# Folding w_phi into wk and wq in groups of six heads instead of row chunks, with a new order of work

## The chip, the cores and the metric

The kernel runs on one core of one Trainium2 chip. A core has TensorE (PE; its weight loads are listed apart as PEld), VectorE (DVE), ScalarE (ACT), GpSimd (POOL) and SyncE (SP), and 16 DMA engines. The metric is the device time of one execution in microseconds. Three executions of the kernel before took 286.2, 286.44 and 286.89 us: a median of 286.44 us.

## The reference, cut to what matters

One token-mixing block and one feed-forward block work on the same x (2048 tokens, D = 640) and are mixed by a gate. The first block is a linear attention with H = 32 heads of Dh = 20 columns:

```
q, k, v = split(x @ wqkv)                          # heads of 20 columns
pq, pk  = q @ w_phi[h],  k @ w_phi[h]              # per head, 20 x 20
phi_q   = [softmax(pq), softmax(-pq)]              # 40 columns a head
phi_k   = [softmax(pk), softmax(-pk)]
kv, z   = sum over tokens of phi_k^T v, of phi_k
a       = (phi_q kv / (phi_q z + 1e-6)) @ wo
b       = (silu(x @ w_gate) * (x @ w_up)) @ w_down # F = 1728
out     = g * a + (1 - g) * b,   g = sigmoid(sum(x * gate_w))
```

Since (x wk) w_phi = x (wk w_phi), with w_phi laid out as a block-diagonal matrix of 32 blocks, the kernel first multiplies wk and wq with w_phi (the "premult") and then needs one projection a token tile in place of two. The change is about this premult.

## The kernel before, in words

Everything is in bf16 with sums in f32. The tokens are 16 tiles of 128 and 4 batches of 4 tiles. The program has no planner at run time: two strings, LOADS and ORDER, list short names of operations, and a loop at the end of `_build` (L849) calls them in that order. Every engine gets its instructions in the order in which they are called; `_Tracker` (L54) adds the semaphore waits that reads and writes of the same bytes need. SP issues nearly all DMAs, in order, and so does ACT for a few.

The names that matter:

- `x`, `t` load token tiles: x0 to x3 as rows, which TensorE transposes (`X`), t4 to t15 by a transposing DMA into xT. `w` loads wv, `f` the FFN weights in three column parts (0 to 256, 256 to 896, 896 to 1728), `h` loads w_phi into the tile wph (from ACT's queue, once the fourth wv load has landed).
- `k0` to `k4`, `q0` to `q4` (`load_wt`, L406) load wk and wq transposed: chunk m is rows 128m to 128m+127 of wqkv, all 640 columns of k (or q), and becomes five blocks [128 columns x 128 rows] in wT (wTq for q).
- `Y` (`w_blocks`, L578) builds the block-diagonal matrix wbd from wph and the mask bmask. As 128 is no multiple of 20, a chunk of 128 rows cuts through heads: each of the five chunks of wbd has 160 columns (8 heads of which some belong partly to the next chunk), and neighbouring chunks overlap. POOL does chunks 0, 2, 4, DVE chunks 1, 3.
- `M0` to `M4` for k and `R0` to `R4` for q (`premult`, L584): six matmuls for a chunk m of rows, one for each entry of BANDS (L573): the weights are a block of wT, 128x128, what moves is a part of wbd, 140 columns in four of the six and 80 in the other two. The result, 640 columns, is copied from PSUM to wqk in one copy: by DVE for M0 and M3, by ACT for the others.
- `V` projects a token tile to v and the gate (`U` is a fifth of a V, for the first three tiles); `K` and `Q` project it to k and q with wqk (10 matmuls of 320 columns), and ACT makes exp(+) and exp(-) of it. A K or a Q reads all five row chunks of wqk, so it needs all five premults.
- `S`, `P` normalise the exponentials of a K tile (DVE: sums and reciprocals; POOL: the multiplication); `E` sums phi_k^T v into two PSUM banks (11 matmuls of 63 columns). `N` ends that sum, `Z` spreads z over all partitions through a DMA to DRAM and back.
- `A`, `B`, `C` (DVE) and `c` (POOL, then a transposing DMA to phiT) turn a Q tile into the scaled phi_q; `O` multiplies two batches of phiT with kv.
- `F b.k` is one 128-column piece of the FFN for batch b: 10 matmuls of 512 columns (F b.13, the last 64 columns, has 10 of 256), and tanh and a copy on ACT, a multiplication on DVE, one on POOL. `D` and `W` are the products with w_down and wo and the store.
- `i3`, `i4` (`fills`, L425) are POOL's memsets of kvsb, eq, qc, hz, hmask and of ph, zh. `I` sets apart two PSUM banks for the sum over k; from then until `N` the PE's results rotate over three pairs of banks, otherwise over four (`next_pair`, L473, takes the pair that was used longest ago).

ORDER interleaves FFN pieces with the attention so that TensorE always has work while the other engines prepare its next operands. At the start only F0.0 and F0.1 can fill, since only the first 256 FFN columns are loaded by then.

Of the kernel before, what the change touches and what calls it, by code (L numbers as in the profile page):

```python
# [30 lines left out]


LOADS = """
x0 w0 x1 g w1 x2 w2 x3 w3 w4 f0 h k0 k1 t4 k2 k3 k4 t5 t6 t7 t8 t9 t10 t11 t12 t13 t14 t15 q0 q1 q2 q3
q4 f1 f2
"""

ORDER = """
H0 H1 H2 H3 H4 H5 H6 H7 H8 H9 H10 H11 H12 X0 G X1 U0.0 U1.0 U0.1 X2 U1.1 U2.0 U0.2 U1.2 U2.1 X3 U2.2
U0.3 U1.3 U2.3 U0.4 U1.4 U2.4 V3 Y F0.1 M1 i3 M0 F0.0 M2 V4 M3 M4 K0 K1 I S0 V6 V5 S1 P0 K3 K2 P1 E0  # L40
V9 K4 E1 S3 V7 P3 K5 S2 V8 V10 S4 P2 P4 E2 R0 E3 K6 S5 P5 S6 i4 E4 V14 K7 K8 P6 V15 S7 R2 E5 K9 S8
P7 R1 E6 K10 S9 V12 P8 E7 P9 K11 S10 P10 F0.2 R3 F1.2 E8 E9 K12 E10 S11 S12 K14 S14 V11 K13 P11 P12
E11 K15 P14 R4 S13 P13 F1.9 S15 P15 E12 V13 T F1.8 E13 F1.11 E14 Q1 E15 Q0 Q2 N A1 A0 Z F2.8 F2.10 J
A2 F0.8 B0 F1.10 C0 c0 F0.7 F0.5 F2.2 B2 F0.9 C2 F1.3 L Q3 F1.4 A3 F3.3 F1.13 c2 B1 F1.12 C1 B3 Q5
F1.7 F2.0 c1 A5 F2.9 F2.6 F3.2 C3 F1.1 c3 Q4 B4 A4 F1.6 F2.3 F2.7 Q6 C4 c4 F0.6 B6 F2.5 B5 F0.3 F3.1
A6 Q7 C5 c5 F3.0 F2.1 C6 c6 F1.0 F0.10 Q8 B7 A7 F1.5 F0.4 C7 c7 B8 Q9 F0.11 F2.11 A8 F2.12 A9 B9
F0.12 Q10 F2.4 F3.4 O0.2 F3.5 C8 A10 c8 F0.13 D0.0 Q11 D0.1 B10 W0 D0.3 C9 A11 C10 c9 c10 B11 Q12
Q13 B12 C11 c11 D0.2 A12 C12 c12 D1.1 Q14 A13 A14 B13 C13 c13 Q15 B14 B15 D1.0 W1 A15 C14 c14 D1.3
C15 c15 D1.2 F3.6 F2.13 F3.7 F3.10 F3.9 F3.12 F3.8 O2.4 F3.11 F3.13 D2.1 D2.0 W2 D2.3 D2.2 D3.0 D3.1
W3 D3.2 D3.3  # L50
"""

# [144 lines left out]
def _build(nc, A_x, A_wqkv, A_w_phi, A_wo, B_x, B_w_gate, B_w_up, B_w_down, gate_w, out):  # L197
    tr = _Tracker(nc)
    pe, act, dve, pool, sp = nc.tensor, nc.scalar, nc.vector, nc.gpsimd, nc.sync
# [81 lines left out]
    wTq = at("wTq", [P, 5, 5, P], BF16, 15872)
    wT = at("wT", [P, 5, 5, P], BF16, 22272)
    wbd = at("wbd", [P, 5, 160], BF16, 28672)
    wph = at("wph", [P, 5, DH], BF16, 30272)
    bmask = at("bmask", [P, 5, 8], BF16, 30528)
    gwr = at("gwr", [P, P], BF16, 30656)
# [15 lines left out]
    def mm(pairs):  # L302
        reads, writes = [], []
        for p in pairs:
            reads += [p[1], p[2]]
            writes.append(p[0])

        def fn():
            last = None
            for o, l, r, st, sp_, sk in pairs:  # L310
                last = pe.matmul(o, lhsT=l, rhs=r, start=st, stop=sp_, skip_group_check=sk)  # L311
            return last
        return run("pe", fn, list({id(a): a for a in reads}.values()), writes)
# [13 lines left out]
    def actop(o, i, func, scale=1.0):  # L327
        rd = [i] + ([scale] if isinstance(scale, bass.AP) else [])
        return run("act", lambda: act.activation(o, i, func, scale=scale), rd, [o])  # L329

    def copy(e, o, i):
        if e == "act":
            return actop(o, i, ACTF.Copy)
        eo = tr.eng[e]
        return run(e, lambda: eo.tensor_copy(o, i), [i], [o])

    def tt(e, o, a, b, op):
        eo = tr.eng[e]
        return run(e, lambda: eo.tensor_tensor(o, a, b, op), [a, b], [o])  # L339
# [15 lines left out]
    def memset(e, a, v):  # L355
        eo = tr.eng[e]
        return run(e, lambda: eo.memset(a, v), [], [a])

    def dma(e, dst, src, transpose=False):
        eo = tr.eng[e]  # L360

        def fn():
            if transpose:
                return eo.dma_start_transpose(dst, src)
# [13 lines left out]
    x2 = A_x[0]  # L378
# [22 lines left out]

    def load_phi():
        tr._wait("act", dict([wv_evs[3]]))
        dma("act", wph[:, :, :], A_w_phi.rearrange("h e f -> (h e) f").rearrange("(c p) f -> p c f", p=P))

    def load_wt(which, m):  # L406
        dst = wT if which else wTq
        dma("sp", dst[:, m, :, :], A_wqkv[m * P:(m + 1) * P, D * which:D * which + D], transpose=True)

    FCUT = [0, 256, 896, F_FFN]  # L410

# [1 line left out]
    select(ident[:, :], [[-1, P]], ALU.not_equal, 1.0, 0, 1)  # L413


    H0 = [0, 6, 12, 19, 25]
    H1 = [7, 13, 20, 26, 32]
    memset("pool", bmask[:, :, :], 1.0)
    for c in range(5):
        b0 = P * c - DH * H0[c]  # L420
        select(bmask[:, c, :], [[-DH, 8]], ALU.is_ge, 0.0, b0, 1)
        select(bmask[:, c, :], [[DH, 8]], ALU.is_gt, 0.0, DH - b0, -1)


    def fills(i):  # L425
# [47 lines left out]
    def next_pair():  # L473
        return used([r for r in ring["lru"] if r < ring["n"] and r not in held][0])
# [59 lines left out]
    def tok_proj(t, which, split=False):  # L534
        pr = next_pair()
        pairs = [(bank(2 * pr + hb, 0, 320), xT[:, t, c, :], wqk[:, which, c, 320 * hb:320 * hb + 320],
                  c == 0, c == 4, False) for c in range(5) for hb in range(2)]
        if split:
            for c in range(5):
                mm(pairs[2 * c:2 * c + 2])  # L540
        else:
            mm(pairs)
        return pr

    def ktile(t):
# [17 lines left out]
    def kvtile(t):  # L563
# [9 lines left out]
    BANDS = [  # L573
        (0, 0, 0, 140, 0), (0, 1, 120, 260, 0), (0, 2, 240, 320, 0),
        (1, 2, 320, 400, 80), (1, 3, 380, 520, 0), (1, 4, 500, 640, 0),
    ]
# [257 lines left out]
    def kv_end():  # L834
# [61 lines left out]
```

## Time and profile before

| what | value |
|---|---|
| median of three executions | 286.44 us |
| the profiled execution, its own time | 286.63 us |
| its span (first to last instruction of the program) | 285.4 us |
| what lies around the span | 1.2 us |
| PE busy | 282.6 us (99%), 1999 matmuls |
| DVE, ACT, POOL busy | 176.0, 146.9, 157.3 us |
| granted TensorE clock | 1.0 in all slices |
| first premult matmul for k, first K tile | at 13.75 us, at 18.85 us |

The trace gives the start of every instruction; a matmul's end is modelled, as matmuls overlap in the array. What a matmul costs the PE is therefore read from the distance between the starts of neighbouring ones, which this document calls its pitch: five matmuls of 512 columns that begin at 11.59 us and are followed at 12.67 us have a pitch of 216 ns, though each is listed with 379 ns. "x12" in a row of the timeline means twelve merged instructions; the text in square brackets is the idle time of the engine before them and what ended it. For a DMA the trace shows the issue on its queue and the landing.

### The profile page before, as it was taken

The page shows a single profiled execution, that of the slowest core. Times are in us where ns is not written, and L with a number is a line of the kernel's source. Part 1 is how long each engine was busy: PE and PEld are TensorE (multiplying, and loading weights), DVE is VectorE, ACT ScalarE, POOL GpSimd, SP SyncE. Part 2 cuts the span into 40 slices and gives each one's busy share as a digit, 9 for nine tenths or more (in the row PEclk, how much of TensorE's full clock was granted, in tenths as well). Part 3 has the DMA queues.
Part 4 walks back from the last instruction along what each step waited for, and adds up shares of the span by engine and source line. Part 5 has one row for each costly group of instructions (what it writes and reads, how often), then busy time and mean ns, then how long its engine had stood idle before and what let it go on. Part 6 is the DMA issues. An engine that isn't in the chain of part 4 may idle for free.

```text
span 285.4 us, 5063 instructions
## 1 busy us (share of the span) xinstructions
PE 282.6 (99%) x1999; PEld 175.1 (61%) x1999; DVE 176.0 (62%) x264; ACT 146.9 (51%) x256; POOL 157.3 (55%) x126
## 2 busy tenths in 40 slices
PE   8999999999999999999999999999999999999997
PEld 7667777575644554444555446767767545767766
DVE  2337748577578959889999849856689647100000
ACT  0668768676665665566657575324241567222022
POOL 8256899879637756978688842561512753200000
PEclk9999999999999999999999999999999999999999
DMA  7988589000010863502222200046344430010011
GB/s 233 198 109 130 102 246 325 6 0 3 2 48 0 231 187 67 103 6 51 51 51 53 51 1 7 7 99 124 80 46 98 80 72 1 9 49 25 23 46 48
DMA packets 49374, 21.87 MB, mean 77 GB/s; under 512 B 39462, under 2 KB 49214, under 8 KB 49350
## 3 DMA queue, kind: packets, MB, share of 16 engines
q1 hardware_dynamic: 47830, 20.67, 31.6%
q10 hardware_dynamic: 1520, 0.87, 1.0%
q8 instruction: 16, 0.26, 0.4%
q14 instruction: 8, 0.07, 0.1%
HBM read 9.38 MB, written 2.62 MB: 42 GB/s over the span
## 4 chain that ended last, share of the span: by engine, by line
PE 99%; DVE 0%; issue 0%
PE ps L311 97%; PE ps L497 1%; PE ps L323 1%; DVE osb L822 0%
## 5 line engine op out<-in xcount | busy, mean ns | idle before, releaser
L311 PE MATMUL ps<-xT,wg 128*128 128x512 bf16 x260 | 64.6, 379 | 0.0
L311 PE MATMUL ps<-xT,wu 128*128 128x512 bf16 x260 | 64.6, 379 | 0.0
L339 POOL TENSOR_TENSOR ph<-eq,qc 128x1320 bf16<-128x1320 bf16 x16 | 40.3, 2517 | 36.2 <-DVE qc L657 27.4
L339 POOL TENSOR_TENSOR hT<-hT,us 128x512 bf16<-128x512 bf16 (+1 forms) x36 | 43.8, 1224 | 24.3 <-DVE hT L343 15.1
L311 PE MATMUL ps<-wqk,xT 128*128 128x320 bf16 x320 | 47.7, 299 | 0.0
L311 PEld LDWEIGHTS ps<-xT,wu 128*128 128x128 bf16 x260 | 25.5, 98 | 30.7
L329 ACT ACTIVATE us<-ps 128x512 bf16<-128x512 f32 (+1 forms) x60 | 34.2, 569 | 19.3 <-PE ps L311 19.1
L339 POOL TENSOR_TENSOR ekr<-ekr,krec 128x1280 bf16<-128x1280 bf16 x16 | 37.3, 2356 | 8.2 <-DVE krec L353 8.2
L311 PEld LDWEIGHTS ps<-xT,wg 128*128 128x128 bf16 x260 | 25.1, 98 | 27.3 <-ACT oT L329 0.6
L329 ACT ACTIVATE osb<-ps,omg 128x640 bf16<-128x640 f32 (+2 forms) x17 | 12.4, 756 | 54.8 <-PE ps L311 54.8
L311 PE MATMUL ps<-wd,hT 128*128 128x320 bf16 (+3 forms) x295 | 40.2, 296 | 0.0
L311 PEld LDWEIGHTS ps<-wqk,xT 128*128 128x128 bf16 x320 | 30.6, 98 | 12.7
L343 DVE SCALAR_TENSOR_TENSOR hT<-hT,ps 128x512 bf16<-128x512 bf16 (+1 forms) x39 | 24.8, 642 | 20.0 <-ACT hT L329 14.4
L311 PEld LDWEIGHTS ps<-wd,hT 128*128 128x128 bf16 (+1 forms) x295 | 26.9, 98 | 11.1 <-issue 1.3
L329 ACT ACTIVATE eq<-ps 128x640 bf16<-128x640 f32 x32 | 22.3, 703 | 17.7 <-PE ps L311 14.0
L339 POOL TENSOR_TENSOR hx<-hx,us 128x512 bf16<-128x512 bf16 (+1 forms) x20 | 23.0, 1159 | 14.2 <-ACT us L329 8.9
L350 DVE TENSOR_REDUCE ksum<-ekr 128x64 f32<-128x1280 bf16 x16 | 23.5, 1470 | 11.6 <-ACT ekr L329 11.6
L329 ACT ACTIVATE hT<-ps 128x512 bf16<-128x512 f32 (+1 forms) x39 | 21.9, 563 | 15.6 <-PE ps L311 11.0
L329 ACT ACTIVATE ekr<-ps 128x640 bf16<-128x640 f32 x32 | 22.3, 703 | 8.7 <-PE ps L311 8.2
L350 DVE TENSOR_REDUCE qz<-eq 128x64 f32<-128x1280 bf16 x16 | 23.6, 1477 | 3.2 <-ACT eq L329 3.2
L311 PE MATMUL ps<-wog,oT 128*128 128x320 bf16 (+2 forms) x165 | 24.7, 295 | 0.0
L311 PE MATMUL ps<-wvg,xT 128*128 128x320 bf16 (+1 forms) x160 | 24.4, 303 | 0.0
(83 smaller groups left out, 285.3 us busy)
## 6 DMA issues: line engine op xcount, KB each, us to landing
out_dram<-osb SPq DMA_DIRECT2D x15, 160.0 KB, 1.8
wd<-in_B_w_down_dram SPq DMA_DIRECT2D x1, 2080.0 KB, 9.1
wg<-in_B_w_gate_dram SPq DMA_DIRECT2D x1, 1040.0 KB, 10.5
wu<-in_B_w_up_dram SPq DMA_DIRECT2D x1, 1040.0 KB, 12.7
wg<-in_B_w_gate_dram SPq DMA_DIRECT2D x1, 800.0 KB, 6.6
wu<-in_B_w_up_dram SPq DMA_DIRECT2D x1, 800.0 KB, 8.2
wog<-in_A_wo_dram SPq DMA_DIRECT2D x2, 375.0 KB, 4.2
xs<-in_A_x_dram ACTq DMA_DIRECT2D x3, 160.0 KB, 4.0
```

Source lines behind the costliest of these rows:

```text
L311: last = pe.matmul(o, lhsT=l, rhs=r, start=st, stop=sp_, skip_group_check=sk)
L323: last = pe.transpose(o, i, ident[0:k, 0:k])
L329: return run("act", lambda: act.activation(o, i, func, scale=scale), rd, [o])
L339: return run(e, lambda: eo.tensor_tensor(o, a, b, op), [a, b], [o])
L343: return run("dve", lambda: dve.scalar_tensor_tensor(out=o, in0=a, scalar=s, in1=b, op0=op0, op1=op1), rd, [o])
L350: return run("dve", lambda: dve.tensor_reduce(o, i, AX.X, ALU.add), [i], [o])
L497: last = pe.matmul(bank(2 * pr, 0, P), lhsT=c, rhs=c, start=True, stop=True)
```

## The change

wk and wq are now loaded in six groups of columns: group c is all 640 rows and the 128 columns from 120c on, of which 120 (six whole heads; 40 in group 5) are used. The transposed group has the 120 head columns on the partitions and the 640 rows of D as five blocks of 128. There is a sixth load for each of wk and wq (k5, q5). w_phi is loaded with 120 rows a group, by two DMAs (five groups, and the rest). wbd has six groups [120 x 120], without overlap, and one mask for all. A premult of group c is five matmuls, one for each block of D rows: weights 120x128, 120 columns moving (40 for group 5), each complete in itself. Its result is a column group of wqk for all five row chunks, 600 elements a partition (200 for group 5); M0, M3 and M5 are copied by DVE, the others by ACT. K0 first does its five matmuls for the first 320 columns, then those for the second. wph, bmask and gwr get memory of their own. ORDER is new from V3 on; it has M5 and R5 in addition and otherwise the same operations.

```
 LOADS = """
-x0 w0 x1 g w1 x2 w2 x3 w3 w4 f0 h k0 k1 t4 k2 k3 k4 t5 t6 t7 t8 t9 t10 t11 t12 t13 t14 t15 q0 q1 q2 q3
-q4 f1 f2
+x0 w0 x1 g w1 x2 w2 x3 w3 w4 f0 h k0 k1 t4 k2 k3 k4 k5 t5 t6 t7 t8 t9 t10 t11 t12 t13 t14 t15 q0 q1 q2 q3 q4 q5
+ f1 f2
 """
 ORDER = """
 H0 H1 H2 H3 H4 H5 H6 H7 H8 H9 H10 H11 H12 X0 G X1 U0.0 U1.0 U0.1 X2 U1.1 U2.0 U0.2 U1.2 U2.1 X3 U2.2
-U0.3 U1.3 U2.3 U0.4 U1.4 U2.4 V3 Y F0.1 M1 i3 M0 F0.0 M2 V4 M3 M4 K0 K1 I S0 V6 V5 S1 P0 K3 K2 P1 E0
-V9 K4 E1 S3 V7 P3 K5 S2 V8 V10 S4 P2 P4 E2 R0 E3 K6 S5 P5 S6 i4 E4 V14 K7 K8 P6 V15 S7 R2 E5 K9 S8
-P7 R1 E6 K10 S9 V12 P8 E7 P9 K11 S10 P10 F0.2 R3 F1.2 E8 E9 K12 E10 S11 S12 K14 S14 V11 K13 P11 P12
-E11 K15 P14 R4 S13 P13 F1.9 S15 P15 E12 V13 T F1.8 E13 F1.11 E14 Q1 E15 Q0 Q2 N A1 A0 Z F2.8 F2.10 J
...
-A6 Q7 C5 c5 F3.0 F2.1 C6 c6 F1.0 F0.10 Q8 B7 A7 F1.5 F0.4 C7 c7 B8 Q9 F0.11 F2.11 A8 F2.12 A9 B9
-F0.12 Q10 F2.4 F3.4 O0.2 F3.5 C8 A10 c8 F0.13 D0.0 Q11 D0.1 B10 W0 D0.3 C9 A11 C10 c9 c10 B11 Q12
...
+U0.3 U1.3 U2.3 U0.4 U1.4 U2.4 V3 Y i4 M0 F0.1 M1 M2 F0.0 M3 M4 V4 I i3 M5 K0 S0 P0 K1 V5 K2 S1 P1 V7
+K3 S2 V9 E0 K4 E1 K5 P2 S3 V10 P3 V12 E2 K6 E3 K7 S4 S5 P4 E4 S6 K8 P5 V6 V8 P6 E5 S7 P7 S8 K9 E6
+V11 P8 K10 R1 E7 S9 P9 K11 E8 S10 P10 K12 S11 P11 F0.6 S12 E9 R2 K13 E10 P12 F1.10 T R5 E11 V14 S13
+P13 K14 F0.3 S14 R0 K15 V13 V15 R4 S15 P14 P15 F1.2 R3 F0.13 E12 E13 E14 Q0 E15 Q1 Q2 N Z A1 A0 A2
...
+F2.9 F3.4 F2.7 A6 Q7 B6 c5 C6 F0.7 A7 F2.5 c6 F1.8 F3.2 F3.0 B7 Q8 Q9 C7 B8 c7 F0.5 A8 F3.1 F0.11 B9
+F2.3 F0.12 O0.2 C8 F2.2 c8 Q10 A9 B10 Q11 D0.1 C9 A10 D0.0 A11 C10 B11 W0 c9 D0.2 c10 Q12 B12 F2.11
...
 def load_phi():
     tr._wait("act", dict([wv_evs[3]]))
-    dma("act", wph[:, :, :], A_w_phi.rearrange("h e f -> (h e) f").rearrange("(c p) f -> p c f", p=P))
+    w = A_w_phi.rearrange("h e f -> (h e) f")
+    dma("act", wph[0:120, 0:5, :], w[0:600, :].rearrange("(c p) f -> p c f", p=120))
+    dma("act", wph[0:40, 5, :], w[600:D, :])
-def load_wt(which, m):
+def load_wt(which, c):
     dst = wT if which else wTq
-    dma("sp", dst[:, m, :, :], A_wqkv[m * P:(m + 1) * P, D * which:D * which + D], transpose=True)
+    c0 = D * which + 120 * c
+    dma("sp", dst[:, c, :, :], A_wqkv[:, c0:c0 + P], transpose=True)
...
-memset("pool", bmask[:, :, :], 1.0)
-for c in range(5):
-    b0 = P * c - DH * H0[c]
-    select(bmask[:, c, :], [[-DH, 8]], ALU.is_ge, 0.0, b0, 1)
-    select(bmask[:, c, :], [[DH, 8]], ALU.is_gt, 0.0, DH - b0, -1)
+memset("pool", bmask[:, :], 1.0)
+select(bmask[:, :], [[-DH, 6]], ALU.is_ge, 0.0, 0, 1)
+select(bmask[:, :], [[DH, 6]], ALU.is_gt, 0.0, DH, -1)
+memset("pool", wph[:, 5, :], 0.0)
...
     if split:
-        for c in range(5):
-            mm(pairs[2 * c:2 * c + 2])
+        for hb in range(2):
+            mm(pairs[hb::2])
...
 def w_blocks():
-    for c in range(5):
-        tt("dve" if c % 2 else "pool", wbd[:, c, :].rearrange("p (h f) -> p h f", f=DH),
-           wph[:, c, :].unsqueeze(1).to_broadcast([P, 8, DH]),
-           bmask[:, c, :].unsqueeze(2).to_broadcast([P, 8, DH]), ALU.mult)
+    for c in range(6):
+        tt("dve" if c % 2 else "pool", wbd[0:120, c, :].rearrange("p (h f) -> p h f", f=DH),
+           wph[0:120, c, :].unsqueeze(1).to_broadcast([120, 6, DH]),
+           bmask[0:120, :].unsqueeze(2).to_broadcast([120, 6, DH]), ALU.mult)
-def premult(which, m):
+def premult(which, c):
     pr = next_pair()
-    pairs = []
-    for i, (hb, c, c0, c1, off) in enumerate(BANDS):
-        o = bank(2 * pr + hb, c0 - 320 * hb, c1 - 320 * hb)
-        pairs.append((o, (wT if which else wTq)[:, m, c, :], wbd[:, c, off:off + c1 - c0], i in (0, 3), i in (2, 5), True))
-    mm(pairs)
-    copy("dve" if which and m in (0, 3) else "act", wqk[:, which, m, :].rearrange("p (b c) -> p b c", b=2), halves(pr))
+    n = min(120, D - 120 * c)
+    c0 = pr * 1024 + 32
+    o = ps[:, c0:c0 + 600].rearrange("p (m j) -> p m j", j=120)[:, :, 0:n]
+    w = wT if which else wTq
+    mm([(o[:, m, :], w[0:120, c, m, :], wbd[0:120, c, 0:n], True, True, False) for m in range(5)])
+    copy("dve" if which and c in (0, 3, 5) else "act", wqk[:, which, :, 120 * c:120 * c + n], o)
```

More of the change, by code (lines that the diff above doesn't have):

```diff
@@ L39 @@
 H0 H1 H2 H3 H4 H5 H6 H7 H8 H9 H10 H11 H12 X0 G X1 U0.0 U1.0 U0.1 X2 U1.1 U2.0 U0.2 U1.2 U2.1 X3 U2.2
-U0.3 U1.3 U2.3 U0.4 U1.4 U2.4 V3 Y F0.1 M1 i3 M0 F0.0 M2 V4 M3 M4 K0 K1 I S0 V6 V5 S1 P0 K3 K2 P1 E0
-V9 K4 E1 S3 V7 P3 K5 S2 V8 V10 S4 P2 P4 E2 R0 E3 K6 S5 P5 S6 i4 E4 V14 K7 K8 P6 V15 S7 R2 E5 K9 S8
-P7 R1 E6 K10 S9 V12 P8 E7 P9 K11 S10 P10 F0.2 R3 F1.2 E8 E9 K12 E10 S11 S12 K14 S14 V11 K13 P11 P12
-E11 K15 P14 R4 S13 P13 F1.9 S15 P15 E12 V13 T F1.8 E13 F1.11 E14 Q1 E15 Q0 Q2 N A1 A0 Z F2.8 F2.10 J
-A2 F0.8 B0 F1.10 C0 c0 F0.7 F0.5 F2.2 B2 F0.9 C2 F1.3 L Q3 F1.4 A3 F3.3 F1.13 c2 B1 F1.12 C1 B3 Q5
-F1.7 F2.0 c1 A5 F2.9 F2.6 F3.2 C3 F1.1 c3 Q4 B4 A4 F1.6 F2.3 F2.7 Q6 C4 c4 F0.6 B6 F2.5 B5 F0.3 F3.1
-A6 Q7 C5 c5 F3.0 F2.1 C6 c6 F1.0 F0.10 Q8 B7 A7 F1.5 F0.4 C7 c7 B8 Q9 F0.11 F2.11 A8 F2.12 A9 B9
-F0.12 Q10 F2.4 F3.4 O0.2 F3.5 C8 A10 c8 F0.13 D0.0 Q11 D0.1 B10 W0 D0.3 C9 A11 C10 c9 c10 B11 Q12
-Q13 B12 C11 c11 D0.2 A12 C12 c12 D1.1 Q14 A13 A14 B13 C13 c13 Q15 B14 B15 D1.0 W1 A15 C14 c14 D1.3
-C15 c15 D1.2 F3.6 F2.13 F3.7 F3.10 F3.9 F3.12 F3.8 O2.4 F3.11 F3.13 D2.1 D2.0 W2 D2.3 D2.2 D3.0 D3.1
+U0.3 U1.3 U2.3 U0.4 U1.4 U2.4 V3 Y i4 M0 F0.1 M1 M2 F0.0 M3 M4 V4 I i3 M5 K0 S0 P0 K1 V5 K2 S1 P1 V7
+K3 S2 V9 E0 K4 E1 K5 P2 S3 V10 P3 V12 E2 K6 E3 K7 S4 S5 P4 E4 S6 K8 P5 V6 V8 P6 E5 S7 P7 S8 K9 E6
+V11 P8 K10 R1 E7 S9 P9 K11 E8 S10 P10 K12 S11 P11 F0.6 S12 E9 R2 K13 E10 P12 F1.10 T R5 E11 V14 S13
+P13 K14 F0.3 S14 R0 K15 V13 V15 R4 S15 P14 P15 F1.2 R3 F0.13 E12 E13 E14 Q0 E15 Q1 Q2 N Z A1 A0 A2
+F2.12 F1.3 J F1.6 B0 F0.8 F2.10 C0 F1.12 L c0 F0.4 F2.1 B1 C1 F1.7 F1.9 Q3 A3 B3 c1 F0.2 F2.0 F0.10
+B2 F1.4 Q4 C2 c2 F2.8 F1.11 C3 F1.5 F2.4 B4 Q5 A4 A5 F2.6 c3 B5 F3.5 F1.0 F3.3 C4 F0.9 F1.1 C5 c4 Q6
+F2.9 F3.4 F2.7 A6 Q7 B6 c5 C6 F0.7 A7 F2.5 c6 F1.8 F3.2 F3.0 B7 Q8 Q9 C7 B8 c7 F0.5 A8 F3.1 F0.11 B9
+F2.3 F0.12 O0.2 C8 F2.2 c8 Q10 A9 B10 Q11 D0.1 C9 A10 D0.0 A11 C10 B11 W0 c9 D0.2 c10 Q12 B12 F2.11
+A12 C11 D0.3 Q13 C12 c11 B13 Q14 c12 F1.13 D1.0 B14 A14 A13 Q15 C14 c14 C13 B15 c13 D1.1 W1 A15 D1.3
+C15 D1.2 c15 F3.10 F2.13 F3.7 F3.11 F3.6 F3.8 O2.4 F3.12 F3.9 D2.0 D2.1 W2 D2.2 D2.3 F3.13 D3.1 D3.0
 W3 D3.2 D3.3
@@ L280, in _build @@
     xs = at("xs", [P, NPE, D], BF16, 10752)
[L281 to L286, printed above, removed]
+    wTq = at("wTq", [P, 6, 5, P], BF16, 15872)
+    wT = at("wT", [P, 6, 5, P], BF16, 23552)
+    wbd = at("wbd", [P, 6, 120], BF16, 31232)
+    wph = sb("wph", [P, 6, DH], BF16)
+    bmask = sb("bmask", [P, 6], BF16)
+    gwr = sb("gwr", [P, P], BF16)
     ps = nc.alloc_psum_tensor("ps", [P, 8 * 512], F32)
@@ L413, in _build @@
     select(ident[:, :], [[-1, P]], ALU.not_equal, 1.0, 0, 1)
-    H0 = [0, 6, 12, 19, 25]
-    H1 = [7, 13, 20, 26, 32]
-    memset("pool", bmask[:, :, :], 1.0)
-    for c in range(5):
-        b0 = P * c - DH * H0[c]
-        select(bmask[:, c, :], [[-DH, 8]], ALU.is_ge, 0.0, b0, 1)
-        select(bmask[:, c, :], [[DH, 8]], ALU.is_gt, 0.0, DH - b0, -1)
+    memset("pool", bmask[:, :], 1.0)
+    select(bmask[:, :], [[-DH, 6]], ALU.is_ge, 0.0, 0, 1)
+    select(bmask[:, :], [[DH, 6]], ALU.is_gt, 0.0, DH, -1)
+    memset("pool", wph[:, 5, :], 0.0)
     def fills(i):
@@ L571, in kvtile @@
         mm(pairs)
[L573 to L576, printed above, removed]
     def w_blocks():
-        for c in range(5):
-            tt("dve" if c % 2 else "pool", wbd[:, c, :].rearrange("p (h f) -> p h f", f=DH),
-               wph[:, c, :].unsqueeze(1).to_broadcast([P, 8, DH]),
-               bmask[:, c, :].unsqueeze(2).to_broadcast([P, 8, DH]), ALU.mult)
-    def premult(which, m):
-        pr = next_pair()
-        pairs = []
-        for i, (hb, c, c0, c1, off) in enumerate(BANDS):
-            o = bank(2 * pr + hb, c0 - 320 * hb, c1 - 320 * hb)
-            pairs.append((o, (wT if which else wTq)[:, m, c, :], wbd[:, c, off:off + c1 - c0], i in (0, 3), i in (2, 5), True))
-        mm(pairs)
-        copy("dve" if which and m in (0, 3) else "act", wqk[:, which, m, :].rearrange("p (b c) -> p b c", b=2), halves(pr))
+        for c in range(6):
[3 more added lines that the diff above has]
+    def premult(which, c):
+        pr = next_pair()
+        n = min(120, D - 120 * c)
[4 more added lines that the diff above has]
+        copy("dve" if which and c in (0, 3, 5) else "act", wqk[:, which, :, 120 * c:120 * c + n], o)
     def kv_finish():
```

## The prediction

> **What bounds the kernel now.** I read the page first, then the timelines of PE, POOL, ACT and SP from the start to the first K tile, then the deadlines of what the change moves. The page's busy times and its chain of what ended last:
>
> ```profile
> PE 282.6 (99%) x1999; PEld 175.1 (61%) x1999; DVE 176.0 (62%) x264; ACT 146.9 (51%) x256; POOL 157.3 (55%) x126
> ...
> PE 99%; DVE 0%; issue 0%
> PE ps L311 97%; PE ps L497 1%; PE ps L323 1%; DVE osb L822 0%
> ```
>
> The chain never leaves PE until the last store. A busy PE need not be at its peak, so I took pitches: 512 columns have 216 ns (below, 1.08 us for five), 320 have 136 ns. That is (216 - 136) / 192 = 0.417 ns a column and 2.7 ns a matmul, and all matmuls from 6 us on keep to it, but for some 0.1 us where the array's shape changes. So **there is no wait left to remove**: a gain must come out of the PE's own work, and every new wait is paid in full. The PE's timeline at the start and around the first E:
>
> ```profile
> 11.59 1.24 PE L311 MATMUL ps<-xT,wg 128*128 128x512 bf16 x5
> 12.67 1.24 PE L311 MATMUL ps<-xT,wu 128*128 128x512 bf16 x5
> 13.75 0.79 PE L311 MATMUL ps<-wbd,wT 128*128 128x140 bf16 x12
> 14.38 1.24 PE L311 MATMUL ps<-xT,wg 128*128 128x512 bf16 x5
> ...
> 16.54 0.48 PE L311 MATMUL ps<-wbd,wT 128*128 128x140 bf16 x6
> 16.85 1.53 PE L311 MATMUL ps<-wvg,xT 128*128 128x320 bf16 x10
> ...
> 27.00 0.51 PE L311 MATMUL ps<-v1r,ekr 128*128 128x63 bf16 x11
> 27.35 1.52 PE L311 MATMUL ps<-wvg,xT 128*128 128x320 bf16 x10
> ```
>
> **Term 1, the premults' own time: -0.20 us.** Twelve matmuls (two premults) take 14.38 - 13.75 = 0.63 us, so ten premults take 3.15. A new group has five matmuls of 120 columns at 120 x 0.417 + 2.7 = 52.7 ns: 264 ns. The sixth has 40 columns; the two figures above make that 19.4 ns, but the eleven of 63 columns show 0.35 us / 11 = 31.4 where they would make 29. I take 31.4, the nearer row. Sum: 2 x (25 x 52.7 + 5 x 31.4) = 2.95 us, 0.20 less; with 19.4 it is 0.32 less. That weights with 120 rows cost nothing extra is read from the z transpose, the one 120*128 operation of before:
>
> ```profile
> 76.83 0.84 PE L311 MATMUL ps<-wqk,xT 128*128 128x320 bf16 x5
> 77.51 0.22 PE L323 MATMUL ps<-ident,zh 120*128 120x120 bf16 x1
> 77.56 1.24 PE L311 MATMUL ps<-xT,wg 128*128 128x512 bf16 x5
> ```
>
> Five K matmuls end at 76.83 + 0.68 = 77.51, where it begins, and its 57 ns are 4 over the rule. The other end: where the shape becomes 120*64 (phiT, below) the start is 0.09 us late. Were that so at both sides of each of twelve premults, they would cost 2.2 us. I take 0.
>
> **Term 2, M0 is moved ahead of F0.1: +0.45 us.** In before F0.1 covers 11.59 to 13.75 while w_phi arrives. Now M0 stands directly behind V3, at 11.59, and waits for wbd's group 0, which POOL makes (POOL's timeline; the bracket is its wait):
>
> ```profile
> 11.39 1.49 POOL L339 TENSOR_TENSOR wbd<-wph,bmask 128x160 bf16<-128x160 bf16 x3 [4.25 <-DMA wph<-in_A_w_phi_dram]
> ```
>
> wph is issued by ACT at 7.36, when the fourth wv load has landed, and lands 4.0 us later; neither gate nor bytes change. Three products of 160 columns take 447 to 583 ns each; for 120 I take 450. Then a hand-over and an uncovered weight load, about 0.1 us each (98 ns is the row of a weight load): 11.39 + 0.45 + 0.2 = 12.04, against 11.59. Bounds: 0.2 us if wph lands 0.25 earlier; nothing if it lands 0.45 earlier; 0.8 if the second w_phi DMA or the transposed loads in flight delay it by 0.35. Behind the waiting M0 stands the whole PE; F0.1's work on the other engines shifts with it. The cover that was there (F0.1) now stands behind.
>
> The Trainium skill ("DMA: Bandwidth & Descriptors", section on why a DMA increments its semaphore by 16) says that a DMA uses the largest number of engines up to 16 that divides its slowest dimension. It speaks against 120 partitions: 15 engines, and 10 for the 40 rows. By it the first load has 600 / 15 = 40 pieces an engine, as the old one had 640 / 16, so that the sum would stay; no run here shows it yet.
>
> **Term 3, the sixth loads on SP: 0, with the smallest margin of all.** Every transposing load holds SP for 1.3 us:
>
> ```profile
> 4.07 4.13 SPq L364 DMA_TRANSPOSE wT<-in_A_wqkv_dram  x2
> 8.24 1.28 SPq L364 DMA_TRANSPOSE xT<-in_A_x_dram  x1
> 9.56 3.92 SPq L364 DMA_TRANSPOSE wT<-in_A_wqkv_dram  x3
> 13.52 16.48 SPq L364 DMA_TRANSPOSE xT<-in_A_x_dram  x11
> 30.04 6.57 SPq L364 DMA_TRANSPOSE wTq<-in_A_wqkv_dram  x5
> ```
>
> k5 takes the place of t5, issued at 13.52 and landed at 18.61 (packets of many loads stood still around 17 us there, beside an instruction fetch). M5 comes at 18.58 by the sum of PE pitches (11.59 + 0.26 + 2.16 + 0.53 + 2.16 + 0.53 + 1.36), with term 2 at 19.03: 0.4 us to spare, less a hand-over. Then K0's second half needs M5's copy: M5 0.16, result 0.2 later, DVE 0.34 (200 of the 640 elements of a 0.82 us copy), hand-over 0.1: 0.80 after M5's start, against 0.16 + 0.68 for K0's first half. It just fits. t5 to t15 come 1.3 us later, q 1.3, f1 and f2 2.6: t5 lands at about 19.9 for V5 at 21.9; f1 at 48.2 for F0.6 at 51.1; f2 at 53.7 for F1.10 at 55.5. All hidden.
>
> What each new load costs is not in the trace: 640 rows of 256 bytes in place of 128 rows of 1280. From below, 1.28 us of SP as now; phiT's transpose of 2.2 times the data has 1.39, so the time is mostly one per instruction. From above, five times 1.28, if each block of 128 rows were an issue of its own. I take 1.28: bytes and blocks are the same, and the packets are 256 bytes already.
>
> The same page (Specifications) asks for transfers of 512 B for line rate, which the new source rows of 256 B miss and the old ones met. If it made these loads 1.3 times as long, k5 would be some 2 us late and the sum 288.3.
>
> **What is off the path.** wbd's six products and two mask instructions instead of ten are POOL and DVE time before or beside wph's wait. The second w_phi issue takes ACT 0.45 us more, out of the 0.71 that ACT idles before its first copy at 9.88. The copies have 600 or 200 elements instead of 640 and hide as now. i4, 3.8 us of POOL at 39.3 amid the P's, moves to 12.9, where POOL is idle: P0 to P11 then need 12 x 2.33 = 28 us from 24.3 on, done by 52.3 where K tiles allow; E11 comes at 57.9. The tightest E is E10: K10 ends at 47.4, then ACT 1.65, S 2.0, P 2.35: 53.4, against 55.2. O0.2 comes 3.7 us earlier (165.6 in place of 169.3) and needs c7's transpose. PE, then SP:
>
> ```profile
> 168.30 1.24 PE L311 MATMUL ps<-xT,wu 128*128 128x512 bf16 x5
> 169.47 2.57 PE L311 MATMUL ps<-phiT,kvsb 120*64 120x512 bf16 x24
> ```
> ```profile
> 160.31 1.37 SPq L364 DMA_TRANSPOSE phiT<-ph  x1
> ```
>
> It lands 3.6 us after issue, 5.6 us ahead of O0.2. Between N and C7 both orders have 32 F pieces and eight A, B and C, which keep DVE busy for 70.1 of 80.5 us; N comes 1.3 us earlier. So 1.9 to 3.2 us remain.
>
> **Sum.** -0.20 + 0.45 + 0 = +0.25 us: 286.63 (span 285.4 and 1.2 around it) becomes 286.88. That execution is 0.19 above the median; on the median it is **286.7 us**. A measurement of this kernel tells about 0.2% (0.57 us) from no change, so this is "the same".
>
> **Rivals.**
> - M0 does not wait (wph lands earlier, or POOL and hand-over are quicker): only term 1 is left, 286.2. For it: nothing on the trace but the spread of one DMA. 0.14.
> - The transposed loads of 640 rows are slower and M5 waits for k5: slower than before. It decides from 0.4 us of delay at k5, 0.07 us a load. At 0.3 us a load k5 comes 1.8 late, 1.4 of it paid: 288.1; at twice the issue time some 6 us: 292.7. For it: k5's place is the one where a landing took 5.1 us. Against: equal packets and bytes. 0.16.
> - w_phi lands over 0.35 us later than before, with two DMAs in place of one: 287.3 to 287.8. 0.07.
> - A wait in the later stages (c7 for O0.2, P for E, a PSUM pair that DVE frees late), about 1 us: 287.7. Margins of 1.8 us and more speak against it. 0.06.
> - Faster by more than 0.2%: needs 0.57 us, and the premults give at most 0.32; only what the profile does not show could bring the rest. 0.05.
>
> The forecast has 0.52. **Chances:** faster 0.05; same 0.52 + 0.14 less 0.04 for a forecast that ends just over the bound, 0.62; slower the rest, 0.33. The range leaves out the slow end of the loads' rival and half of the fast case: 285.9 to 288.3.
>
> **What the profile after would show.** Term 1: the wbd,wT rows as five at 53 ns a pitch, 12 premults in 2.95 us. Term 2: POOL's first wbd at 11.4 and the first premult near 12.0, with idle time of PEld before it. Term 3: SP's rows for wT 1.3 us each, k5 landing by 19.0, no gap before M5 and K0. F0.6, F1.10, O0.2 start where the sums put them, plus 0.45. It is wrong if the chain of waits names a DMA of wT or xT, or phiT.

## The result, and the profile after

| | before | after |
|---|---|---|
| median, 22 executions of each | 286.62 us | 286.99 us |
| lowest and highest | 286.16, 287.88 us | 286.66, 289.02 us |
| the profiled execution, its span | 286.63, 285.4 us | 287.37, 286.1 us |
| start of the last matmul | 283.24 us | 284.02 us |
| first K tile (K0) | 18.85 us | 19.75 us |

The medians differ by +0.37 us (0.13%), where +0.25 was forecast. The ratio of all executions is 1.0023 [1.0012, 1.0034], 0.66 us; it stands near the ratio of the means (287.26 and 286.62 us), which the upper tail of after draws away from the medians: 5 of its 22 executions take over 287.5 us, 1 of before's 22. So the change is a small loss, by the one measure under the 0.2% of the prediction and by the other just over it. The two profiled executions differ by 0.74 us; the one of after lies 0.38 above its median.

The page of the kernel after, busy times, the queue of w_phi (it had 1520 packets in before) and the chain of what ended last:

```profile
PE 282.2 (99%) x1999; PEld 174.6 (61%) x1999; DVE 178.9 (63%) x266; ACT 147.7 (52%) x257; POOL 156.8 (55%) x119
...
q10 hardware_dynamic: 1529, 0.87, 1.0%
...
PE 93%; SPq 4%; DMA 2%; issue 0%; DVE 0%
PE ps L311 93%; SPq L364 3%; DMA wT<-in_A_wqkv_dram 2%; SPq L365 1%; DVE osb L818 0%; PE ps L323 0%
```

PE's share did not move, 99%, and yet the chain is another: in before it stayed on the PE, now it goes through SP (4%) and a load of wT (2%) before it comes to the PE. That is the sign that the prediction named as its own refutation. The chain in order of time shows where (start, duration, what):

```profile
11.14 1.27 SPq L364
12.41 0.04 issue
12.46 5.48 DMA wT<-in_A_wqkv_dram
17.93 0.05 issue
17.98 59.40 PE ps L311 x576
```

SP issues k4 at 12.46, it lands at 17.93, and M4 begins at 17.98. From there the PE runs on without a break until the first change of the array's shape. The PE's timeline of after at the start:

```profile
12.34 0.42 PE L311 MATMUL ps<-wbd,wT 120*128 120x120 bf16 x5 [0.96 <-issue]
12.60 1.25 PE L311 MATMUL ps<-xT,wg 128*128 128x512 bf16 x5
13.68 1.24 PE L311 MATMUL ps<-xT,wu 128*128 128x512 bf16 x5
14.76 0.69 PE L311 MATMUL ps<-wbd,wT 120*128 120x120 bf16 x10
15.29 1.25 PE L311 MATMUL ps<-xT,wg 128*128 128x512 bf16 x5
16.37 1.24 PE L311 MATMUL ps<-xT,wu 128*128 128x512 bf16 x5
17.45 0.97 PE L311 MATMUL ps<-wbd,wT 120*128 120x120 bf16 x10
18.25 1.53 PE L311 MATMUL ps<-wvg,xT 128*128 128x320 bf16 x10
19.62 0.28 PE L311 MATMUL ps<-wbd,wT 120*128 120x40 bf16 x5
19.75 1.52 PE L311 MATMUL ps<-wqk,xT 128*128 128x320 bf16 x10
```

Three things are to be read here. M0 stands at 12.34 with idle time before it; "issue" is no cause, the bracket only says that no semaphore event was found for the end of the wait. M1 and M2 take 15.29 - 14.76 = 0.53 us. M3 and M4, the same ten matmuls, begin at 17.45, but V4 follows only at 18.25, 0.80 later: the missing 0.27 us lie before M4.

In pitches, from after's V3 to the end:

| piece | after against before |
|---|---|
| V3 ends at 11.22 instead of 11.59 | -0.37 |
| M0 waits after V3 (before: F0.1 follows at once) | +1.13 |
| M0 to M5 take 1.44 instead of 1.57 | -0.13 |
| M4 waits for k4 | +0.27 |
| K0 at 19.75 instead of 18.85 | **+0.90** |
| R0 to R5, again | -0.13 |
| last matmul, 284.02 instead of 283.24 | **+0.78** |

The first row is not the change: in before four V matmuls at 5.1 to 5.9 us stood 0.47 us too wide, in after they did not. It helped nothing, since M0 waits for w_phi wherever V3 ends. So M0 stands 0.75 us later than F0.1 stood in before (12.34 against 11.59), and this is what Term 2 had put at 0.45.

Why 12.34 and not 12.04: the fourth wv load, the gate, landed at 7.64 instead of 7.33, and so ACT issued w_phi at 7.66. ACT's and POOL's timelines of after:

```profile
7.66 1.01 ACTq L365 DMA_DIRECT2D wph<-in_A_w_phi_dram  x2
```
```profile
11.77 1.24 POOL L339 TENSOR_TENSOR wbd<-wph,bmask 120x120 bf16<-120x120 bf16 x3 [6.21 <-DMA wph<-in_A_w_phi_dram]
```

It landed at 11.69, 4.0 us after its issue as before. POOL's start is 0.38 later than in before, and 0.31 of that is the gate's; from there to M0 it is 0.58 us (the first product, 0.47, and the hand-over), where 0.65 was predicted. That it is this product that M0 waits for, and not a pair of PSUM banks, is seen across kernels: in the three profiles where M0 waits in the same way (after, and below the wide warm-up and q0 ahead) it begins 0.58 us after POOL's start each time, though POOL starts anywhere from 11.77 to 12.41.

SP's queue, too, was late before the loads in question. The first two loads of wk hold it for 4.41 us, where in before they held it for 4.13, and so k2 to k4 are issued 0.26 to 0.27 us later:

```profile
4.05 4.41 SPq L364 DMA_TRANSPOSE wT<-in_A_wqkv_dram  x2
```

### The profile page after: what moved, and what is told of

It reads as the page before. It is cut to its first block, busy times and chain, and to the rows that moved or that the text cites. A ratio compares the mean times of both kernels' runs of the same rounds, so it can differ in the third digit from the quotient of the medians.

```text
span 286.1 us, 5059 instructions
## 1 busy us (share of the span) xinstructions
PE 282.2 (99%) x1999; PEld 174.6 (61%) x1999; DVE 178.9 (63%) x266; ACT 147.7 (52%) x257; POOL 156.8 (55%) x119
## 4 chain that ended last, share of the span: by engine, by line
PE 93%; SPq 4%; DMA 2%; issue 0%; DVE 0%
PE ps L311 93%; SPq L364 3%; DMA wT<-in_A_wqkv_dram 2%; SPq L365 1%; DVE osb L818 0%; PE ps L323 0%
## 5 line engine op out<-in xcount | busy, mean ns | idle before, releaser
L339 POOL TENSOR_TENSOR hT<-hT,us 128x512 bf16<-128x512 bf16 (+1 forms) x36 | 42.2, 1177 | 48.1 <-DVE hT L343 36.1
L339 POOL TENSOR_TENSOR ph<-eq,qc 128x1320 bf16<-128x1320 bf16 x16 | 41.5, 2592 | 22.3 <-DVE qc L653 20.2
L329 ACT ACTIVATE osb<-ps,omg 128x640 bf16<-128x640 f32 (+2 forms) x17 | 12.5, 757 | 56.0 <-PE ps L311 56.0
L339 POOL TENSOR_TENSOR hx<-hx,us 128x512 bf16<-128x512 bf16 (+1 forms) x20 | 24.7, 1239 | 24.2 <-DVE hx L343 23.8
L311 PE MATMUL ps<-wvg,xT 128*128 128x320 bf16 (+1 forms) x160 | 23.8, 300 | 0.0
```

## The theories, and the experiments

Two questions were open. **What does the wait cost?** Theory A: M0's wait for w_phi is only the first of two gates in a row. The second is SP's queue of transposing loads (1.3 us each), whose last ones land hardly before M2 to M5 ask for them; so taking away the first wait uncovers the second and gives back only a part, and any load put ahead of the last k loads is paid. Theory B: the k loads have room, the cost is M0's wait alone. **Why did the k loads take so long?** k3, k4 and k5 took 5.3 to 5.5 us in after; k2, k3 and k4 took 3.5 to 3.6 in before (the tile's view of wT in before, then in after; the largest value in each is k0's):

```profile
DMA to landing us min/median/max: 3.5/3.6/6.2
```
```profile
DMA to landing us min/median/max: 3.6/5.3/6.4
```

Theory F: the first big instruction fetch of the PE's program fell among them. Theory G: their new shape (640 rows of 256 bytes) is slower. The DMA view of the stretch 13.5 to 14.5 us, before, then after, shows what F rests on: the queue q8, of kind instruction, has a packet there in after alone (in before it comes at 16.50), and the rest of the traffic falls from 547 packets to 354.

```profile
q1 hardware_dynamic: 547, 0.14, 73.3%
```
```profile
q1 hardware_dynamic: 354, 0.09, 51.2%
q8 instruction: 1, 0.02, 11.0%
```

All kernels below compute the whole reference. Each ratio is against runs of before on the same chip.

### F0.1 back in front of M0

```
-V3 Y i4 M0 F0.1 M1 M2 F0.0 M3 M4 ...
+V3 Y i4 F0.1 M0 M1 M2 F0.0 M3 M4 ...
```

> The changed kernel with one move undone: F0.1 stands ahead of M0 again, so that it covers the arrival of w_phi. In the changed kernel the PE waits 1.13 us before M0 and 0.27 us before M4. Theory A (the loads of wk set the time of the first K tile; M0's wait lies beside them): M0's wait goes, but the PE then waits for k3 to k5, about 1 us before M3, M4 or M5; K0 begins between 19.2 and 19.8 us as now (19.75); time within 0.3 us of the changed kernel, 1.001 to 1.003 of before. Theory B (the wait for w_phi is the whole price): no wait at M3 to M5, K0 at about 18.5 us, time 0.8 to 1.1 us less than the changed kernel, 0.998 to 0.999 of before.

Measured: median 286.65 us (12 executions, 286.10 to 288.21), ratio 1.0007 [0.9990, 1.0024]. The wait at M0 is gone. The PE's timeline of this kernel:

```profile
13.54 0.69 PE L311 MATMUL ps<-wbd,wT 120*128 120x120 bf16 x10
14.58 0.44 PE L311 MATMUL ps<-wbd,wT 120*128 120x120 bf16 x5 [0.35 <-DMA wT<-in_A_wqkv_dram]
...
17.56 0.44 PE L311 MATMUL ps<-wbd,wT 120*128 120x120 bf16 x5 [0.38 <-DMA wT<-in_A_wqkv_dram]
18.80 0.44 PE L311 MATMUL ps<-wbd,wT 120*128 120x120 bf16 x5 [0.81 <-DMA wT<-in_A_wqkv_dram]
```

M2, M3 and M4 now wait for k2, k3 and k4: 0.51, 0.55 and 0.97 us in pitches, and K0 comes at 20.57. That execution is the highest of its twelve (the gate landed at 8.06, k2 was issued 1.1 us later than in after), so its sum is no measure, but its place is: the second gate is there. The median is 0.34 below after's. The two ran on different chips; against the runs of before beside each, after stands 0.37 above and this kernel 0.04 below, so 0.41 apart. That is about a third of the 1.13 that M0 waited in after's profile, and lies between what A (within 0.3) and B (0.8 to 1.1) expected. The intervals of the two ratios overlap, so this run alone doesn't settle the size of the gain.

### w_phi without its gate

```
 def load_phi():
-    tr._wait("act", dict([wv_evs[3]]))
```

> The changed kernel with w_phi's two DMAs issued by ACT at once, at about 3.2 us, not after the fourth wv load; M0 still stands ahead of F0.1. wph then lands at 7 to 9 us and wbd is ready long before V3 ends, so that M0 waits for nothing. Theory A: the PE reaches M3 to M5 1.1 us sooner and waits there for k3 to k5 as in the run with F0.1 first; K0 at 19.0 to 19.8 us; 0.0 to 0.6 us less than the changed kernel, 0.9995 to 1.001 of before. Theory B: K0 at 18.4 to 18.7, 1.1 us less than the changed kernel, 0.9975 to 0.9985 of before. Both: the wv loads may land up to 0.3 us later behind the w_phi pieces.

Measured: median 286.47 (286.19 to 287.50), ratio 1.0000 [0.9988, 1.0013], 0.52 below after (0.41, again, with each taken against its own runs of before). w_phi is issued at 3.18 and lands at 9.33. The PE's timeline:

```profile
11.60 0.43 PE L311 MATMUL ps<-wbd,wT 120*128 120x120 bf16 x5
...
17.24 1.53 PE L311 MATMUL ps<-wvg,xT 128*128 128x320 bf16 x10
18.77 0.29 PE L311 MATMUL ps<-wbd,wT 120*128 120x40 bf16 x5
18.91 2.33 PE L311 MATMUL ps<-wqk,xT 128*128 128x320 bf16 x16
```

M0 follows V3 at once. V4 ends at 18.60 (17.24 + 1.36) and M5 begins at 18.77: 0.16 of wait, for k5, which landed at 18.72. K0 at 18.91 lies between the places of A (19.0 to 19.8) and of B (18.4 to 18.7). This is the smallest edit that takes Term 2 away, and no slowdown is left that can be measured; the two intervals just touch (this one ends at 1.0013, after's begins at 1.0012). It isn't faster than before either: K0 stands at 18.91, 0.06 later than in before though M0 to M5 save 0.13 ahead of it, as the wait for k5 takes that. Of the 0.26 us of Term 1 the last matmul shows 0.06 (283.18 against 283.24).

### A load of q ahead of k4

```
-... k2 k3 k4 k5 t5 ...
+... k2 k3 q0 k4 k5 t5 ...
```

> The changed kernel with the load q0 moved from behind t15 to between k3 and k4: the same work, but one transposing load more (1.3 us of SP) ahead of k4 and k5. The trace of the run with F0.1 first had shown waits at M1, M4 and M5 as soon as M0's wait was gone. Theory A (the last loads of wk set K0): k4 and k5 land 1.3 us later, the PE waits 1.3 to 1.6 us at M4 (it waited 0.27) and perhaps 0.3 more at M5, K0 begins at 20.8 to 21.3 us; 0.9 to 1.4 us more than the changed kernel, 1.004 to 1.007 of before. Theory B (the w_phi wait is the whole price and k4, k5 have room): no change against the changed kernel, 1.001 to 1.002 of before.

Measured: median 287.87 (287.07 to 289.10), ratio 1.0046 [1.0031, 1.0062], 0.88 above after. The PE's timeline:

```profile
17.75 0.43 PE L311 MATMUL ps<-wbd,wT 120*128 120x120 bf16 x5
18.55 0.44 PE L311 MATMUL ps<-wbd,wT 120*128 120x120 bf16 x5 [0.38 <-DMA wT<-in_A_wqkv_dram]
18.82 1.53 PE L311 MATMUL ps<-wvg,xT 128*128 128x320 bf16 x10
20.19 0.28 PE L311 MATMUL ps<-wbd,wT 120*128 120x40 bf16 x5
20.32 0.97 PE L311 MATMUL ps<-wqk,xT 128*128 128x320 bf16 x6
```

M4 waits 0.54 us for k4, issued at 14.27 and landed at 18.50. B, which expected no change, does not fit: one more load on SP costs 0.66 us by the ratios and 0.99 by the medians, each against its own runs of before, half to three quarters of its 1.3 us. The place, M4, is A's; the wait there and K0 at 20.32 are smaller than A expected, because the loads took 4.2 us here and not 5.4. Of the 0.57 us by which K0 is later than in after's profile only 0.27 lie at M4; 0.30 lie at M0 already, as the gate landed at 8.02 in this execution. So the profile shows where the load is paid, but not the whole of what the medians show.

### The new groups in the old order, and the new order with the old premults

The first has after's code with before's ORDER, M5 put behind M4 and R5 behind R3; the second has before's code with after's ORDER, without M5 and R5.

> The groups of six heads with the order of before: M5 put behind M4, R5 behind R3, nothing else. It shows the price of the grouped loads and premults without the new order. Theory A: no wait for w_phi (F0.1 stands first), but M5 comes at about 18.2 us and k5 lands at 17.5 or, if an instruction fetch of the PE falls among the loads of wk, at 19.0; K0 at 18.4 to 19.3 us; 0.999 to 1.002 of before. Theory B: no wait at all, only the 0.26 us that the premults save: 0.999 of before.

> The row chunks of before (five loads, six matmuls a premult) in the new order, without M5 and R5. Here M0 needs all five products of wbd, the last of which was ready at 12.9 us in before, and nothing fills ahead of it. Both theories: M0 waits until 13.0 to 13.4 us, 1.4 to 1.8 us, and k4 landed at 15.75 in before, long ahead of M4's place at 18, so nothing gives the wait back: 1.004 to 1.007 of before. If M0's wait were free for some other reason than the wk loads, it would be 1.000.

The groups alone: median 286.84 (286.50 to 288.10), ratio 1.0007 [0.9990, 1.0024]. V3 ends 0.26 earlier than in before, K0 begins only 0.09 earlier, at 18.76: 0.23 us of wait for k5 at M5 and 0.07 at K0 are more than the premults' 0.13. Later there is one wait that neither before nor after has, in pitches 0.45 us:

```profile
53.90 1.24 PE L311 MATMUL ps<-xT,wg 128*128 128x512 bf16 x5 [0.29 <-ACT us L329]
```

R5 is one more user of the three pairs of banks, and by the rotation the pair that comes next is F0.2's, which ACT has not yet read out (the bracket names ACT's instruction). So the sixth group is not free in the old order either: k5 and R5 take back what the premults save.

The order alone: median 288.16 (288.03 to 290.63, 8 executions), ratio 1.0064 [1.0039, 1.0089]: the worst of all. An old premult needs all five chunks of wbd, and POOL's last product ends only near 13.0. M0 waits 2.05 us in pitches:

```profile
13.10 0.47 PE L311 MATMUL ps<-wbd,wT 128*128 128x140 bf16 x6 [1.88 <-POOL wbd L339]
```

All of it is paid, K0 is at 20.35, as nothing waits for a load there (k4 landed at 15.14). So the new groups are what makes the new order bearable: with them M0 needs one product, with the old premult all five.

### Can the fetch be moved?

Two kernels were to shift the fetch and nothing else: one with 13 warm-up matmuls of 256 columns in place of 26 of 128, one with 48 fulfilled waits on the PE ahead of M0.

> The changed kernel with the PE's 26 warm-up matmuls of 128 columns replaced by 13 of 256: the same columns, 26 instructions fewer ahead of all others on the PE's stream, so that the first 16 KB instruction fetch of the PE (at 13.86 us in the changed kernel, among the loads of k3, k4 and k5, whose landings took 5.3 to 5.5 us; at 16.5 in before, behind them, with landings of 3.5) falls 1 to 2.5 us later. Theory F (the fetch holds up the transposing loads): k3 and k4 land 3.6 us after issue, at 14.8 and 16.1, M4's wait of 0.27 goes; M0's wait of 1.1 stays; 0.2 to 0.3 us less than the changed kernel, 1.000 to 1.002 of before. Theory G (it is the new shape of the loads that makes them slow): k3 and k4 still land 5.3 us after issue wherever the fetch falls, and M4 waits as now.

> The changed kernel with 48 waits that are long fulfilled put on the PE's stream ahead of M0: they cost the sequencer time that lies beside M0's wait of 1.1 us, and push all later instructions 48 places on, so that the 16 KB instruction fetch comes earlier in the program, at 10 to 12.5 us in place of 13.9. Theory F (transposing loads in flight during the fetch are held up): the slow landings (over 4 us) move to the loads issued before about 12.5 us (t4, k2, k3), and k4 and k5 land 2.9 to 3.7 us after issue; M4's wait goes or stays under 0.1. Theory G (k3 to k5 are slow for another reason, such as where they stand behind the first loads): k3, k4, k5 land 5.3 us after issue as in the changed kernel. If the fetch does not move, this tells nothing. Time 286.7 to 287.2, 1.000 to 1.002 of before, under both.

Neither moved it. With the wide warm-up it came at 14.20 us, 1.2 after M0 (1.5 in after), where 1 to 2.5 us later than in after was expected; with the waits at 13.81, where 10 to 12.5 was. So both miss their purpose, and as tests of F they are inconclusive. Medians: 287.22 (286.85 to 287.91, ratio 1.0015 [1.0002, 1.0029]) and 287.58 (287.10 to 289.06, six executions, ratio 1.0043 [1.0022, 1.0064]). The first has M0's wait (1.2 us) and none at M4, for k4 took 4.2 us and M0 was late. The profile of the second shows M0's wait, now with the right name in the bracket, and no wait at M4 either:

```profile
12.63 0.42 PE L311 MATMUL ps<-wbd,wT 120*128 120x120 bf16 x5 [1.10 <-POOL wbd L339]
```

That its median is 0.6 us above after is not explained by this. Neither kernel lies below after, though both profiles lack the wait at M4: what that wait is worth in a median is not shown.

What does tell F from G is the fetch and the landings of all profiles side by side (us; issue to landing of the transposing loads; from the packet and landing records):

| kernel | first fetch at | loads around it | the k loads away from it |
|---|---|---|---|
| before | 16.50 | t5, t6, t7: 5.1, 4.6, 4.2 | k2, k3, k4: 3.6, 3.5, 3.5 |
| after | 13.86 | k3, k4, k5: 5.3, 5.5, 5.3 | k2: 3.6 |
| groups in the old order | 12.63 | k2, k3, k4: 4.5, 4.2, 4.6 | k5: 3.8 |
| old premults, new order | 15.60 | t5, t6: 4.6, 3.8 | k2, k3, k4: 3.3, 3.3, 2.9 |
| q0 ahead | 14.18 | k3, q0, k4: 4.3, 4.1, 4.2 | k5: 3.4 |
| w_phi without gate | 14.06 | k3, k4, k5: 4.7, 4.1, 4.7 | k2: 3.8 |

For these loads G falls: x tiles, old in shape, are about as slow when the fetch comes among them, and the q loads, new in shape, are quick where none does (the tile's view of wTq in after; q0, q2 and q3 take 2.9 to 3.1 and q1 3.7, while q4 and q5, in flight at the third fetch, at 39.45, take 4.3 and 3.7):

```profile
DMA to landing us min/median/max: 2.9/3.4/4.3
```

F fits all eleven profiles, the five that the table leaves out too, and the second fetch (t12 to t14 in after: 4.3, 3.9, 3.8), but as the fetch could not be moved by itself, it is a regular coincidence and not a proof. The fetch's own packet took 1.7 to 1.8 us in the three profiles with the slowest k loads (after, F0.1 in front, the 48 waits: 5.0 to 5.5) and 0.9 to 1.3 in the others, so that both may be slowed by something else. What sets its time stays open. Nor is a fetch the only thing that goes with slow loads: k0, k1 and t4, issued from 4 to 9.3 us while the first weights are still arriving, take 3.6 to 7.2 us in every profile with no fetch near.

For k0, though, the shape may matter. In the two profiles with row chunks k0 holds SP for 2.6 us and lands 6.1 to 6.2 after its issue; in all nine with groups it holds SP for 3.0 to 3.8 and lands 6.4 to 7.2 after its issue, and k2 is issued 0.3 to 1.6 us later. No experiment here loads k0 in its old shape into the new kernel.

### A better version?

Two kernels split K0 and K1 into their halves of 320 columns (operation j), so that a half which needs no M5 can cover the wait for k5. The first builds on the kernel with F0.1 in front, the second on the one without w_phi's gate:

```
+... V3 Y i4 F0.1 M0 M1 M2 F0.0 j0.0 V4 M3 M4 M5 j1.0 j0.1 I i3 S0 P0 j1.1 V5 ...
```
```
+... V3 Y i4 M0 F0.1 M1 M2 F0.0 M3 M4 V4 j0.0 M5 j1.0 j0.1 I i3 S0 P0 j1.1 V5 ...
```

> The kernel with F0.1 first, and the first halves of K0 and K1 (columns 0 to 319, which need the groups 0 to 2 alone) taken out and put ahead of V4 and behind M5: 0.68 us of PE work more ahead of the groups that arrive last, and 0.68 us beside the copy of M5. Theory A: M5's place moves from 18.2 to 18.9 us, so the wait for k5 shrinks to 0 to 0.5 us where the loads are undisturbed; 0.3 to 0.7 us less than with F0.1 first alone, 0.998 to 1.000 of before, the first version that keeps the 0.26 us of the premults. If a PSUM pair or M5's copy binds instead, a wait of 0.3 to 0.5 us stands before the half of K1 or the second half of K0, and the time is that of the run with F0.1 first.

> The two gains put together: w_phi issued at once, as in the run with the ungated w_phi (286.47 against 286.51 of before, a wait of 0.16 us left before M5), and the first half of K0 between V4 and M5, the first half of K1 behind M5, but in an order in which each of M5 and the halves finds its PSUM pair long free (in the earlier run with halves V4's copy held M5 for 0.58 us). Theory A: M5's place moves by 0.68 us to 19.3, behind k5's landing in most executions; no wait over 0.1 us from 6 to 25 us; 0.2 to 0.5 us less than the ungated run, 0.998 to 0.9995 of before. If the half tiles bring a new wait (K1's exponentials behind K0's on ACT, and V5 or K2 for a pair), the time is that of the ungated run, 1.000.

The first: 287.01 (286.41 to 289.03), ratio 1.0014 [0.9993, 1.0036]. It has 0.58 us of wait at M5, for a pair of banks and no longer for a load:

```profile
20.11 0.28 PE L311 MATMUL ps<-wbd,wT 120*128 120x40 bf16 x5 [0.42 <-ACT svec L329]
```

The second: 286.85 (286.24 to 288.03), ratio 1.0011 [0.9996, 1.0026], where less than 1 was expected. Its profiled execution has 286.31 us, and one wait:

```profile
16.93 0.44 PE L311 MATMUL ps<-wbd,wT 120*128 120x120 bf16 x5 [0.24 <-DMA wT<-in_A_wqkv_dram]
```

M0 comes at 11.14, 1.20 earlier than in after, M4 at 16.93, no earlier than k4 lets it: SP issues it at 12.46, just as in after, and it lands at 16.88. The wait for k5 is covered, the one for k4 is not: what is gained on the PE's side meets the same queue. No kernel here is shown to beat before.

## Why the prediction was right, and where not

**The sign and the size were right** in the medians, +0.37 where +0.25 was forecast, and part of that may be luck: no execution near the median was profiled, and in the one that was two terms of the sum are larger than predicted. For this execution, 286.88 against 287.37, the 0.49 come out of the three terms (-0.06 + 0.30 + 0.27 = 0.51):

- **Term 1** (-0.20) was a little too small: -0.26. The 120 columns have 52.8 ns (52.7 predicted). The 40 columns have 26 ns; I had taken 31.4 from the row of 63 columns, with 19.4 as the other end. Weights of 120 rows cost nothing, as read off the z transpose.
- **Term 2** (+0.45) had the right mechanism and the wrong size: +0.75. Each duration of it held. What failed is its start, "neither gate nor bytes change": the gate is the landing of a load, and over the profiles it fell between 7.30 and 8.33 us. In after's it was 0.31 later than in the trace that I summed from, and with it w_phi, POOL and M0. This need not be chance: the two kernels with row chunks have the gate at 7.33 and 7.30, the nine with groups at 7.48 to 8.33, and k0 in its new shape is in flight beside it. So "the gate does not change" was an assumption; whether the change itself moved the gate is not settled by two profiles. The kernel without the gate shows the cause of the slowdown: without this wait none is left to measure (1.0000 [0.9988, 1.0013]), as with F0.1 in front (1.0007 [0.9990, 1.0024]).
- **Term 3** (0, "the smallest margin of all") is the step that failed: 0.27 us at M4. The margin was worked out for k5 alone, with a landing of 5.1 us beside the fetch. For k3 and k4 I made no sum at all; with the 3.5 us of before they would have been in time, but the fetch came 2.6 us earlier and all three took over 5. k4 was also issued 0.26 us later than in before, by k0 and k1: I had put every load at 1.3 us of SP, though the row that I showed has 4.13 us for these two. Had either of the two delays been absent, M4 would by these numbers have waited for next to nothing (12.20 + 5.48 = 17.68, or 12.46 + 3.55 = 16.01, against 17.71, where M3 ends). k5 itself was harmless, it landed at 19.05 and M5 begins at 19.62; k4, one place up, was late.

**The rivals.** "M0 does not wait" did not happen. "The transposed loads are slower and M5 waits" was half right: they were slower and their path did end last, but for k3 to k5 the shape is not the likely reason, and the wait was at M4. "w_phi lands over 0.35 us later", given 0.07, happened in the profiled execution, 11.69 against 11.32, with a time in its range (287.37 of 287.3 to 287.8); its reason, the second DMA, did not: 0.30 of the 0.37 is the later issue behind the gate. The median, 286.99, stays below that range. "A wait in the later stages" did not come: from K0 to the end after has only the 0.09 to 0.13 us at each change of the array's shape that before has too. F0.6 (51.66), F1.10 (56.13) and O0.2 all stand without a gap; around O0.2, where c7's transpose had the margin of 1.9 to 3.2 us:

```profile
165.56 1.24 PE L311 MATMUL ps<-xT,wu 128*128 128x512 bf16 x5
166.73 2.58 PE L311 MATMUL ps<-phiT,kvsb 120*64 120x512 bf16 x24
```

**The two rules weighed.** The row of queue q10 has 9 packets more than in before. The Trainium skill ("DMA: Bandwidth & Descriptors", section on why a DMA increments its semaphore by 16) would have it so: one signal for each engine used, 15 + 10 in place of 16. It cost nothing that shows here, w_phi landed 4.0 us after issue both times. The same page's other rule (Specifications), that transfers under 512 B miss line rate, is not tested by this case: the transposing loads move in packets of 256 B in both kernels, whatever the length of the source rows. Away from a fetch the q loads take 2.9 to 3.7 us in after and 2.9 to 3.5 in before.

**What stays open.** The 0.41 us by which each of the two kernels without M0's wait lies below after (medians, each against its own runs of before) are less than that wait; A names where the rest goes in their profiled executions, but each of these is one of twelve. Of 22 executions of after 5 take over 287.5 us, and 8 of 101 of before; late loads in those are a guess, as they were not profiled.

## What to carry to other kernels

Where the PE has no wait left, the first use of a late operand must stay behind its cover: moved ahead of it, the PE waits for what is left of the operand's path, from the gate that starts its load on. A faster PE piece is worth only what the slowest serial queue behind it allows; here 0.26 us of matmul time were bought with one more 1.3 us issue on SP, and the next load on the same queue cost 0.7 to 1.0. A margin taken from one trace should be checked for every load of the queue, with the slowest landing that the trace shows anywhere, and not for the last one alone.

## What the runs showed of the hardware

- A matmul of 40 columns has a pitch of 26 ns and one of 63 columns 31.4; the line through 320 and 512 columns would make 19 for 40, so it does not hold down there.
- Queue q8 moves 16 packets of 16 KB, one for about every 256 of the PE's 4105 instructions in after (matmuls and weight loads), which is why it is taken for the fetch of the PE's program. Around each of the first two, two or three transposing loads take 3.8 to 5.5 us; most others issued between 9.5 and 30 us take 2.8 to 3.8. That the fetch causes it is not shown.
- The landing of the same early load (the fourth of wv) differs by 1.0 us between the eleven profiles, 7.30 to 8.33, and what is gated by it moves as a whole. The two earliest are those of the two kernels with row chunks.
- A DMA of 120 partitions with 600 pieces took ACT 0.66 us to issue in after, and one of 40 rows 0.31; the single one of 128 partitions in before had 0.44.
